# A linear-attention and feed-forward kernel: two cumulative sums a unit instead of three, decays computed two units ahead, and a new order of casts in the ramp

## The chip, the cores and the metric

The kernel runs on one core of a Trainium2 chip. The metric is the device time of one execution in microseconds (us), as the median of several executions. A profile is one execution seen by the hardware profiler. Its engines are PE (TensorE, matrix products), DVE (VectorE), ACT (ScalarE), POOL (GpSimd) and SP, whose queue issues the DMA transfers. Each engine works through its own queue in order. PEld is PE's loading of weights, and the *granted clock* is the share of full speed that PE was granted in the record. In the kernels the results of PE land in tiles of PSUM, and the other tiles lie in SBUF; an *eviction* is an instruction that copies a tile from PSUM to SBUF.

## The reference, cut to what matters

A recurrent attention with a decay per channel is followed by a feed-forward layer with a tanh-gelu. There are 4 batches, 8 heads, 768 steps and a head width of 48.

```python
for t in range(S):                               # r, k, v, w: [4, 8, 768, 48]
    cur = einsum('bhd,bhe->bhde', u[None] * kt, vt)
    y[:, :, t] = einsum('bhd,bhde->bhe', rt, state + cur)
    state = wt[:, :, :, None] * state + einsum('bhd,bhe->bhde', kt, vt)
x = y.transpose(0, 2, 1, 3).reshape(3072, 384)
return gelu_tanh(x @ w_in) @ w_out               # w_in 384 x 2048, w_out 2048 x 384
```

## The kernel before

The work is cut into 12 *units*. A unit is 256 steps of one batch, and two neighbouring steps share a partition. A unit's attention turns the logarithms of the decays into cumulative sums (a matrix product with a triangular matrix), and these into factors by Exp. It multiplies k and r by the factors, transposes both on PE, and forms masked scores, outputs and a new state. Its feed-forward part is an *up-projection* (`mm1`: eight groups of six 256-column matmuls, each group followed by a gelu) and a *down-projection* (`mm2`: two halves of sixteen 384-column matmuls). The attention of unit q+1 is a Python generator whose steps (`next(att)`) are placed between the matmuls of unit q. The preparation of a unit's factors and of its scaled k and r (`kk`, `rq`) is placed at the end of a pass of the loop. POOL prepares `rk` (the product of k, r and u), `vb` (v in bf16), `vsc` (`vb` scaled) and `am` (a block mask scaled by the unit's decay). How many units ahead of its use a preparation is made I call its *lead*; it is one here.

```python
def a1(q):                                # cumulative sums: three for the two steps of a partition
    x, y, z = (ps_a.tile([P, 512], FP, tag="a", name=f"cum{q}_{i}") for i in range(3))
    for dst, s0, s1 in ((x, strict, strict), (y, incl, strict), (z, incl, incl)):
        PE.matmul(dst[:, 0:HD], s0, lw[:, 0, :, 0:D], start=True, stop=False)
        PE.matmul(dst[:, 0:HD], s1, lw[:, 1, :, 0:D], start=False, stop=True)
    ...
def exps(q): ...                          # four Exps of 384 columns, one small one for al
def prep(q):
    DVE.tensor_tensor(out=kk[:, :, :, 0:D], in0=tdh(kt), in1=dec(e1), op=AL.mult)   # 768 columns
    DVE.tensor_tensor(out=rq[:, :, :, 0:D], in0=tdh(rt), in1=dec(fq), op=AL.mult)   # 768 columns
    POOL.tensor_copy(out=vb, in_=tdh(vt))
    POOL.tensor_tensor(out=rk, ...k, r...); POOL.tensor_tensor(out=rk, ...rk, u_bc...)
    for c2 in range(2):
        POOL.tensor_tensor(out=am[:, c2], in0=blk..., in1=al..., op=AL.mult)
def prep_b(q):                            # dg: DVE reduces rk; vsc: POOL multiplies vb by dg
    ...
def a2(q, which):                         # eight PE transposes, then one DVE copy PSUM -> SBUF (TT)
    ...
# ---- ramp (cut): casts of w_in between the steps of attention(0); a1/exps/prep of unit 1 after them
for q in range(NU):
    if q + 3 < NU: load(q + 3, "k"), ...  # loads are issued at the start of the pass
    att = attention(q + 1) ...
    table("gelu")
    if ramp:                              # q < 2: all up-projections first
        for i in range(8): mm1(q, i)
        if q == 0:
            for i in range(8):            # the eight casts of w_out, in one go, over three engines
                cast_w_out(i, DVE if i in (0, 3, 6) else (ACT if i in (1, 4, 7) else POOL))
    for i in range(8):
        if not ramp: mm1(q, i)
        if i >= 2: mm2(q, 0, (2 * i - 4, 2 * i - 3))
        if i in (1, 3, 4, 5, 6, 7): next(att, None)
        if i == 6 and 0 < q and q + 2 < NU: a1(q + 2)
    table("exp")
    ...
    exps(q + 2); ln(q + 3)
    mm2(q, 0, range(12, 16)); ...; store(q, 0)
    prep(q + 2); prep_b(q + 2)            # for the transposes of the next pass
    mm2(q, 1, range(8)); ...; mm2(q, 1, range(8, 16)); store(q, 1)
```

## Time and profile before

The time before is 236.3 us (median of 3 runs, 235.0 to 237.8). The table lists when each unit starts, read from PE's timeline at its first up-projection matmul.

| unit | 1 | 2 | 3 | 4 | 5 | 6 | 7 | 8 | 9 | 10 | 11 | 12 | end |
|---|---|---|---|---|---|---|---|---|---|---|---|---|---|
| start, us | 24.8 | 53.7 | 74.0 | 91.3 | 107.9 | 124.5 | 141.0 | 157.6 | 173.8 | 190.1 | 206.3 | 220.6 | 235.9 |

I call units 1 to 3 the ramp. From unit 4 to unit 9 a unit takes 16.2 to 16.6 us. The page of the kernel before has each engine's busy time and share. It then gives the share of each of 40 equal slices in tenths, and PE's granted clock in tenths:

```profile
span 235.9 us, 5759 instructions
PE 203.4 (86%) x2448; PEld 143.0 (61%) x2448; DVE 131.3 (56%) x211; ACT 134.0 (57%) x223; POOL 104.5 (44%) x87
...
PE   0456787598895999999999999999999999999992
PEclk9999996779997999999999999999999999999998
```

PE is full from the fourteenth slice on; before it, its clock dips twice. The view by stages confirms this. Its columns are the stretch, its length, the busy us and instructions of PE, PEld, DVE, ACT and POOL, then PE's granted clock, and last what the DMA engines did. The two lines are the first unit and the six units from the fourth:

```profile
24.80:53.70 28.90, 21.52 (x209) 13.47 (x207) 19.91 (x21) 16.41 (x27) 18.37 (x14) 0.82 0.80 212
91.30:190.10 98.80, 95.41 (x1235) 68.55 (x1233) 58.94 (x93) 63.12 (x111) 49.31 (x36) 1.00 0.52 117
```

In these six units PE is busy 95.4 of 98.8 us and DVE 58.9 us, which is 9.8 us a unit. The timeline around the start of the seventh unit shows the order on DVE and POOL. Its columns are start, length, engine and line, operation, and the idle time before it with what ended that:

```profile
140.26 0.96 DVE L202 TENSOR_TENSOR kk_126<-k_1635,e_2184 128x768 bf16<-128x768 f32 x1 [0.61 <-ACT e_2184 L184]
...
141.14 0.95 DVE L203 TENSOR_TENSOR rq_128<-r_1637,fq_2183 128x768 bf16<-128x768 f32 x1
141.15 2.42 POOL L215 TENSOR_TENSOR am_2216<-blk,al_2185 128x384 f32<-128x384 bf16 x2 [8.26 <-ACT al_2185 L187]
...
143.34 0.68 DVE L238 COPY TT_1_2278<-T_1_2269 128x1024 bf16<-128x1024 bf16 x1
...
143.75 0.81 PE L345 MATMUL h_2_2291<-xT_2203,w_in_sb 128*128 128x256 bf16 x6 [0.36 <-ACT g_2252 L347]
```

DVE multiplies k and r in 0.95 us each, at once. POOL's two `am` multiplies begin with the second of them and take 2.42 us. In the first unit, where DVE does not multiply two SBUF tiles beside it, each of the pair takes 0.82 us, 1.61 together. The eviction `TT_1` starts 0.4 us after its transposes, behind one copy. PE waits 0.36 us, for a gelu.

### The profile page before, as it was taken

What the parts mean: (1) busy time and instruction counts of PE and PEld (TensorE: products, weight loads), DVE (VectorE), ACT (ScalarE), POOL (GpSimd) and SP (SyncE); (2) the same over time, 40 slices, a digit from 0 to 9 for tenths busy, and PEclk for the clock granted to TensorE, in tenths of its full rate; (3) what the DMA queues carried; (4) which work ended last, traced back from release to release, by engine and by line L of the source; (5) the groups of instructions that cost most, each with busy time, mean ns of one, the idle gap of its engine ahead of it and who ended that gap; (6) DMA issues with size and microseconds to landing.
All of it is one profiled execution on the core that took longest, in us unless ns stands there. A gap on an engine that the chain in (4) does not pass through costs nothing.

```text
span 235.9 us, 5759 instructions
## 1 busy us (share of the span) xinstructions
PE 203.4 (86%) x2448; PEld 143.0 (61%) x2448; DVE 131.3 (56%) x211; ACT 134.0 (57%) x223; POOL 104.5 (44%) x87
## 2 busy tenths in 40 slices
PE   0456787598895999999999999999999999999992
PEld 0334564357564767667767667676777677677761
DVE  7684686561636538547547747656285376374200
ACT  3433780566255449459368377395494684765670
POOL 3473792639008504806708509329158076060000
PEclk9999996779997999999999999999999999999998
DMA  7999999713902911942923914915719120020202
GB/s 173 307 396 297 331 320 255 160 33 72 231 15 54 246 25 36 206 98 53 232 56 75 257 24 111 210 33 124 182 35 212 24 62 10 13 56 0 68 1 67
DMA packets 56969, 30.45 MB, mean 129 GB/s; under 512 B 50928, under 2 KB 56176, under 8 KB 56944
## 3 DMA queue, kind: packets, MB, share of 16 engines
q1 hardware_dynamic: 56944, 30.09, 52.1%
q8 instruction: 19, 0.31, 0.6%
q14 instruction: 6, 0.05, 0.1%
HBM read 25.36 MB, written 4.72 MB: 127 GB/s over the span
## 4 chain that ended last, share of the span: by engine, by line
PE 54%; ACT 19%; DVE 11%; issue 9%; POOL 3%; DMA 2%; DVEq 0%; ACTq 0%; POOLq 0%
ACT L156 5%; DVE w_out_sb L86 2%; DMA w_89<-in_w_dram 2%; PE o_0_532 L354 1%; DVE rq_127 L203 1%; ACT logw_124 L162 1%; PE o_0_3678 L354 1%; PE o_0_3457 L354 1%; PE o_0_3175 L354 1%; PE o_1_3740 L354 1%; PE o_1_3632 L354 1%; PE o_1_3389 L354 1%; POOL rk_418 L210 1%; POOL rk_418 L212 1%; ACT logw_122 L162 1%
## 5 line engine op out<-in xcount | busy, mean ns | idle before, releaser
L345 PEld LDWEIGHTS <-w_in_sb 128*128 128x128 bf16 x576 | 54.0, 99 | 21.1 <-issue 9.9
L156 ACT ACT_TABLE_LOAD x13 | 16.7, 1283 | 0.9 <-PEq L487 0.7
L158 ACT ACT_TABLE_LOAD x12 | 15.4, 1283 | 0.2
L171 PEld LDWEIGHTS <-strict 128*128 128x128 bf16 x24 | 2.5, 104 | 9.9 <-issue 9.5
L215 POOL TENSOR_TENSOR am_997<-blk,al_975 128x384 f32<-128x384 bf16 x2 | 2.4, 1230 | 12.5 <-ACT al_975 L187 12.5
L215 POOL TENSOR_TENSOR am_1304<-blk,al_1273 128x384 f32<-128x384 bf16 x2 | 2.4, 1229 | 11.5 <-ACT al_1273 L187 11.5
L215 POOL TENSOR_TENSOR am_1608<-blk,al_1577 128x384 f32<-128x384 bf16 x2 | 2.4, 1230 | 8.3 <-ACT al_1577 L187 8.3
L215 POOL TENSOR_TENSOR am_1912<-blk,al_1881 128x384 f32<-128x384 bf16 x2 | 2.4, 1230 | 8.3 <-ACT al_1881 L187 8.3
L215 POOL TENSOR_TENSOR am_2216<-blk,al_2185 128x384 f32<-128x384 bf16 x2 | 2.4, 1230 | 8.3 <-ACT al_2185 L187 8.3
L215 POOL TENSOR_TENSOR am_2520<-blk,al_2489 128x384 f32<-128x384 bf16 x2 | 2.4, 1228 | 8.3 <-ACT al_2489 L187 8.3
L215 POOL TENSOR_TENSOR am_2811<-blk,al_2780 128x384 f32<-128x384 bf16 x2 | 2.4, 1228 | 7.9 <-ACT al_2780 L187 7.9
L215 POOL TENSOR_TENSOR am_3100<-blk,al_3069 128x384 f32<-128x384 bf16 x2 | 2.4, 1228 | 7.9 <-ACT al_3069 L187 7.9
L215 POOL TENSOR_TENSOR am_3382<-blk,al_3352 128x384 f32<-128x384 bf16 x2 | 2.4, 1228 | 7.9 <-ACT al_3352 L187 7.9
L354 PE MATMUL o_0_532<-w_out_sb,g_437 128*128 128x384 bf16 x16 | 5.5, 469 | 0.2 <-ACT w_out_sb L84 0.2
L236 PEld LDWEIGHTS <-rq_127 128*128 128x128 bf16 x48 | 3.4, 104 | 3.3 <-DVE rq_127 L203 3.2
L354 PEld LDWEIGHTS <-g_437 128*128 128x128 bf16 x32 | 3.3, 117 | 3.2 <-issue 2.5
L170 PE MATMUL cum_0_201<-logw_122,strict 128*128 128x384 bf16 x1 | 0.5, 479 | 5.4 <-ACT logw_122 L162 5.4
L362 DVE COPY ob_3736<-o_0_3678 128x384 f32<-128x384 f32 x1 | 0.6, 558 | 7.7 <-PE o_0_3678 L354 7.7
L215 POOL TENSOR_TENSOR am_699<-blk,al_677 128x384 f32<-128x384 bf16 x2 | 2.3, 1187 | 4.3 <-ACT al_677 L187 4.3
L354 PEld LDWEIGHTS <-g_3653 128*128 128x128 bf16 x32 | 3.0, 98 | 1.7 <-ACT g_3653 L347 0.4
L238 DVE COPY TT_1_818<-T_1_809 128x1024 bf16<-128x1024 bf16 x1 | 0.7, 692 | 6.0 <-PE T_1_809 L236 6.0
L354 PE MATMUL o_0_3678<-w_out_sb,g_3653 128*128 128x384 bf16 x16 | 3.8, 327 | 0.0
(942 smaller groups left out, 694.2 us busy)
## 6 DMA issues: line engine op xcount, KB each, us to landing
wi_155<-in_moe_w_in_dram SPq DMA_DIRECT2D x1, 512.0 KB, 5.0
wi_157<-in_moe_w_in_dram SPq DMA_DIRECT2D x1, 512.0 KB, 6.0
wi_159<-in_moe_w_in_dram SPq DMA_DIRECT2D x1, 512.0 KB, 6.7
wi_161<-in_moe_w_in_dram SPq DMA_DIRECT2D x1, 512.0 KB, 7.5
wi_163<-in_moe_w_in_dram SPq DMA_DIRECT2D x1, 512.0 KB, 8.7
wi_165<-in_moe_w_in_dram SPq DMA_DIRECT2D x1, 512.0 KB, 9.6
w_89<-in_w_dram SPq DMA_DIRECT2D x1, 384.0 KB, 3.7
k_91<-in_k_dram SPq DMA_DIRECT2D x1, 384.0 KB, 4.7
```

The lines of the kernel that those rows point to most:

```text
L86: eng.tensor_copy(out=out, in_=in_)
L156: ACT.preload_act_table_set(EXP_SET)
L158: ACT.preload_act_table(AF.Gelu_apprx_tanh)
L162: ACT.activation(out=lw[:, :, :, 0:D].rearrange("p t h d -> p h t d"), in_=ld.pop(("w", q)).rearrange("p h (t d) -> p h t d", t=2), func=A ...
L171: PE.matmul(dst[:, 0:HD], s1, lw[:, 1, :, 0:D], start=False, stop=True)
L203: DVE.tensor_tensor(out=rq[:, :, :, 0:D], in0=tdh(rt), in1=dec(fq), op=AL.mult)
L210: POOL.tensor_tensor(out=rk, in0=kt.rearrange("p h (t d) -> p h t d", t=2), in1=rt.rearrange("p h (t d) -> p h t d", t=2), op=AL.mult)
L212: POOL.tensor_tensor(out=rk, in0=rk, in1=u_bc[:, :, None, :].broadcast_to([P, H, 2, D]), op=AL.mult)
L215: POOL.tensor_tensor(out=am[:, c2], in0=blk.rearrange("p g j d -> p g (j d)"), in1=al[:, :, c2][:, :, None].broadcast_to([P, G, 2 * D]), o ...
L236: PE.transpose(ps[:, g, :, t2, :], src[:, t2, ds(2 * g, 2), :], ident)
L345: PE.matmul(h[:, f, :], w_in_sb[:, cb, ts(ft, P)], xT[:, cb, :], start=(f + cb == 0), stop=(cb == NCB - 1), skip_group_check=True)
L354: PE.matmul(st["o", q, c2], g[:, ft, ts(c2, P)], w_out_sb[:, ft, :], start=(ft == 0), stop=(ft == NFT - 1))
```

## The change

The intent is less work a unit and a smoother ramp. The factor between the two steps of a partition is multiplied into k and r directly (`kw`, `rw`), so two cumulative sums and two Exps of 384 columns suffice. Each of the two 768-column multiplies becomes two of 384, and two more make `kw` and `rw`. Decays and preparation run two units ahead, not one. The transposes come right after the first up-projection group. The casts of `w_out` are strung out between PE's work in the first unit, and loads of k, r and v are issued after a unit's stores. The diff, cut to its core:

```diff
-        x, y, z = (ps_a.tile(...) for i in range(3))
-        for dst, s0, s1 in ((x, strict, strict), (y, incl, strict), (z, incl, incl)):
+        x, z = ((pool or ps_a).tile(...) for i in range(2))
+        for dst, tri in ((x, strict), (z, incl)):
...
+    def prep_w(q):
+        DVE.tensor_tensor(out=kw, in0=kt[:, :, 0:D], in1=wt[:, :, D:2 * D], op=AL.mult)
+        DVE.tensor_tensor(out=rw, in0=rt[:, :, D:2 * D], in1=wt[:, :, 0:D], op=AL.mult)
+    def prep_a(q):                       # POOL: rk, rk, and v's cast (on ACT for the first unit)
...
     def prep(q):
-        DVE.tensor_tensor(out=kk[:, :, :, 0:D], in0=tdh(kt), in1=dec(e1), op=AL.mult)
-        DVE.tensor_tensor(out=rq[:, :, :, 0:D], in0=tdh(rt), in1=dec(fq), op=AL.mult)
+        for dst, t2, x, dec in ((kk, 0, kw, e1), (kk, 1, kt[:, :, D:2 * D], e1),
+                                (rq, 0, rt[:, :, 0:D], fq), (rq, 1, rw, fq)):
+            DVE.tensor_tensor(out=dst[:, :, t2, :, 0:D], in0=gjd(x), in1=dec..., op=AL.mult)
...
+    for q in range(3):                   # the ramp: six up-projection groups, transposes, two more
+        ...
+        table("exp")
+        if q == 0: wo(0)                 # wo(i) casts a part of w_out, on ACT and DVE in turn
+        mm2(q, 0, (0, 1))
+        next(att)
+        if q == 0: wo(1)
+        mm2(q, 0, (2, 3))
+        next(att)
+        if q == 0: prep_b(1); wo(2); wo(3)
+        mm2(q, 0, range(4, 8))
+        ...                              # and so on to wo(7)
+    for q in range(3, NU):
+        att = attention(q + 1) if q + 1 < NU else iter(())
+        table("gelu")
+        n = q + 3
+        for i in range(8):
+            mm1(q, i)
+            if i >= 4: mm2(q, 0, (2 * i - 8, 2 * i - 7))
+            if i in (0, 1, 2, 4, 5, 6, 7): next(att, None)
+            if q == 3 and i == 0: prep_a(5)
+            if q == 3 and i == 3: prep_w(5); prep(5); prep_b(5)
+            if n < NU:
+                if i == (4 if q == 3 else 0): prep_a(n)
+                if i == 5: prep_w(n)
+                if i == 6: a1(n); prep_b(n)
+        table("exp")
+        if n < NU: exps(n)
+        ...
+        store(q, 0)
+        if n < NU: prep(n)
+        mm2(q, 1, range(16))
+        store(q, 1)
+        krv(q + 4)                       # loads of k, r, v, behind the stores
```

In code `q` and `n` count from 0, in the text units count from 1.

## The prediction

> **What bounds it now.** Two regimes. (1) From the fourth unit on, TensorE: the timeline shows first up-projection matmuls at 124.5, 141.0 and 157.6 us, a period of 16.56 us, and the table of windows has PE busy 15.8 of 16.5 us. I sum about 15.9 us of issue in one unit: 5.2 up-projection, 5.2 down-projection, 0.9 transposes of k and r, 1.65 cumulative sums, the rest attention. Sixteen down-projection matmuls of 384 columns take 2.60 us, 163 ns each; the Trainium skill ("TensorE: Matmul & The Clock Gate", Back-to-back issue gap) gives N/2.4+2.5 = 162.5 ns, so PE runs warm and tight. Remaining gaps in the timeline: about 0.5 us where the third up-projection waits for the first gelu behind exp, ln and a table load, and 0.31 us where a cumulative sum waits for ScalarE to free a PSUM buffer. (2) The first 91 us (first up-projection at 24.8 us, fourth unit at 91.3) are a dependency chain across all engines: only three units in 66.5 us.
>
> **What changes, costed.** Steady unit: two cumulative sums instead of three remove two 384-column matmuls (0.32 us PE); the Exps fall from four to two (2 x 0.38 us ScalarE), so ScalarE reaches the first gelu before PE needs it and the 0.5 us gap goes. But the transposes now stand between the first and second up-projection, so the score matmuls wait for VectorE's two 0.68 us evictions: I estimate a new 0.5 us gap. The PSUM wait stays. VectorE gains about 1 us a unit, off the path. Period about 15.95 us: -0.55 us for six units.
>
> Decays two units ahead move one unit's sums and exps from the late stage into the ramp: the last two overlapped units run at about 14.6 us.
>
> Ramp: all weight casts of w_in come after the first attention; w_out casts follow the gelus and the exp table load, then alternate with the mask multiplies on VectorE, and PE's in-order queue waits for each. In the first unit v's cast on ScalarE holds up the first exps until v lands (9.0 us). I add up: first gelu about 28.4 us (27.6 before), second unit starts near 58.5 us (53.7), third 75.7 (74.0), fourth 93 (91.3). VectorE multiplies of two SBUF inputs block behind GpSimd (the skill, "SBUF — State Buffer", Summary: rules for kernel authors): one took 2.56 instead of 0.95 us at 26.35 us. The extra multiplies enlarge this in the ramp.
>
> **Sum.** 93 + 6 x 15.95 + 2 x 14.6 + 15.1 = 233 us of span, 233.5 us of time, 1.2% faster. Range 229.5 to 238.5. Chances: faster by over 2% 0.25, within 2% 0.67, slower 0.08.
>
> **What would show each step.** PE's timeline: period 15.8 to 16.1 us; no wait for gelu before the third up-projection, but a wait of score matmuls on VectorE's eviction; second cumulative sum waiting on ScalarE's xs. Fourth unit starts at 91 to 95 us; second unit later than before. Windows: VectorE busy about 11 us per unit, ScalarE about 0.8 us less.
>
> **What would make it wrong.** The ramp: it is a long chain; if VectorE and GpSimd collide less or casts arrive earlier, the fourth unit could start at 88 us and the result pass -2%. If loads of k, r, v, now issued after the stores, land too late, steady units gain nothing.

## The result, and the profile after

The changed kernel takes 261.1 us (median of 4 fast runs, 260.1 to 262.4), the kernel before 236.1 us (235.0 to 237.8) in the same rounds. The ratio is 1.1055, with a 95% interval from 1.097 to 1.114: 10.6% slower. A ratio here is always the mean time of one kernel's runs over that of the other's of the same rounds, so it is not quite the ratio of the medians.

```profile
span 258.4 us, 5726 instructions
PE 202.6 (78%) x2424; PEld 143.5 (56%) x2424; DVE 173.8 (67%) x261; ACT 126.5 (49%) x201; POOL 101.7 (39%) x84
...
PE   1264684547999989939899597798896996999993
PEclk9999996555999999977999999799999999999998
```

The totals of PE, ACT and POOL fell a little; that of DVE rose by 42.5 us with only 50 more instructions. The starts of the units tell where the span went:

| unit | 1 | 2 | 3 | 4 | 5 | 6 | 7 | 8 | 9 | 10 | 11 | 12 | end |
|---|---|---|---|---|---|---|---|---|---|---|---|---|---|
| start, us | 28.0 | 66.7 | 83.4 | 100.2 | 123.0 | 139.4 | 157.8 | 177.6 | 194.7 | 212.4 | 228.6 | 243.2 | 258.4 |
| its unit takes | 38.7 | 16.7 | 16.8 | 22.8 | 16.4 | 18.4 | 19.8 | 17.1 | 17.7 | 16.2 | 14.6 | 15.2 | |
| longer than before | 9.8 | -3.6 | -0.5 | 6.2 | -0.2 | 1.9 | 3.2 | 0.9 | 1.4 | 0.0 | 0.3 | -0.1 | |

The last row and the 3.2 us of the later first start add up to the 22.5 us. There are four places.

**The first unit (+9.8 us).** The view by stages for the first unit, the fourth, and the fifth to ninth:

```profile
28.00:66.70 38.70, 25.70 (x215) 15.62 (x215) 15.82 (x24) 16.44 (x26) 10.54 (x9) 0.69 0.65 177
...
100.20:123.00 22.80, 17.94 (x207) 12.51 (x206) 22.12 (x27) 10.54 (x17) 17.69 (x13) 0.85 0.37 83
123.00:212.40 89.40, 77.17 (x1017) 56.85 (x1015) 73.51 (x97) 48.27 (x79) 42.16 (x30) 0.98 0.47 106
```

In the first unit no engine but PE is busy for half the time, and PE's clock averages 0.69. PE's timeline has the waits in it:

```profile
40.56 0.48 PE L376 MATMUL o_0_526<-w_out_sb,g_437 128*128 128x384 bf16 x2 [2.84 <-ACT w_out_sb L84]
...
43.24 0.80 PE L376 MATMUL o_0_526<-w_out_sb,g_437 128*128 128x384 bf16 x2 [1.84 <-DVE w_out_sb L86]
...
47.32 0.80 PE L376 MATMUL o_0_526<-w_out_sb,g_437 128*128 128x384 bf16 x2 [1.95 <-DVE w_out_sb L86]
...
53.81 0.80 PE L376 MATMUL o_0_526<-w_out_sb,g_437 128*128 128x384 bf16 x2 [2.91 <-DVE w_out_sb L86]
```

The first down-projection waits for a cast again and again. A cast stands in DVE's queue behind mask multiplies that need PE's score matmuls, and those stand in PE's queue behind the down-projection that needs the cast before. The two engines take turns. The two 384-column matmuls at 43.24 end 0.80 us after the first began, against 0.48 us at 40.56: the clock has fallen. PE is busy 4.2 us longer than in the kernel before (25.70 for 21.52) and idle 5.6 us longer; `e6` below shows what the slower matmuls have to do with it.

**The fourth unit (+6.2 us).** Its pass holds two preparations: the sixth unit's, and that of the seventh. DVE is busy 22.1 of its 22.8 us. In DVE's timeline six multiplies of the sixth unit stand in front of the state update of the fifth:

```profile
106.81 1.17 DVE L188 TENSOR_TENSOR rw_1471<-r_1061,w_766 128x384 f32<-128x384 f32 x1
107.90 1.18 DVE L236 TENSOR_TENSOR kk_127<-kw_1470,e_1309 128x384 bf16<-128x384 f32 x1
...
112.48 1.57 DVE L327 TENSOR_TENSOR S_0_1552<-tmp_0_1553,am_1332 128x384 bf16<-128x384 f32 x1
```

PE waits for that `S_0_1552` for 4.6 us, up to 114.10. Four of the six multiplies take 1.16 to 1.18 us, where 0.55 us is what they take undisturbed.

**The fifth to ninth unit (+7.2 us).** DVE is busy 73.5 us in these five units, 14.7 us a unit against 9.8 before. A look at 152 us shows what the added time is:

```profile
152.42 2.01 POOL L197 TENSOR_TENSOR rk_2030<-rk_2030,u_bc 128x768 f32<-128x768 f32 x1
154.37 1.15 POOL L86 CAST vb_2029<-v_1993 128x768 bf16<-128x768 f32 x1
...
152.68 2.16 DVE L187 TENSOR_TENSOR kw_2191<-k_1989,w_1690 128x384 f32<-128x384 f32 x1
154.76 1.17 DVE L188 TENSOR_TENSOR rw_2192<-r_1991,w_1690 128x384 f32<-128x384 f32 x1
```

The same `kw` multiply takes 0.55 us in the units where POOL is idle beside it (`kw_740`, at 67.4 us). Here it ends 0.41 us after POOL's multiply ended, and `rw` 0.41 us after POOL's cast ended. POOL's cast takes 1.15 us against 0.82 us elsewhere in the same trace. The two queues block each other in turn: in these lines each multiply pays for one GpSimd instruction. This is the rule of the Trainium skill, "SBUF — State Buffer", Summary: rules for kernel authors: when VectorE "has two SBUF inputs while the GpSimd op reads SBUF, the second one to issue **fully blocks** until the first finishes". The trace agrees. Note that it shows the block as a long instruction, 2.16 for 0.55 us, not as a wait.

What PE sees of it comes at the start of the next unit, 157.8 us:

```profile
157.65 1.22 DVE L236 TENSOR_TENSOR kk_127<-kw_2191,e_2249 128x384 bf16<-128x384 f32 x1
...
158.41 2.24 POOL L241 TENSOR_TENSOR am_2271<-blk,al_2250 128x384 f32<-128x384 bf16 x2
...
158.79 1.18 DVE L236 TENSOR_TENSOR kk_127<-k_1989,e_2249 128x384 bf16<-128x384 f32 x1
...
159.89 1.18 DVE L236 TENSOR_TENSOR rq_128<-r_1991,fq_2248 128x384 bf16<-128x384 f32 x1
...
161.00 0.55 DVE L236 TENSOR_TENSOR rq_128<-rw_2192,fq_2248 128x384 bf16<-128x384 f32 x1
...
162.53 0.68 DVE L254 COPY TT_1_2323<-T_1_2324 128x1024 bf16<-128x1024 bf16 x1
...
163.26 0.24 PE L271 MATMUL mt_0_0_2347<-TT_1_2323,TT_0_2312 48*64 48x128 bf16 x2 [3.10 <-DVE TT_1_2323 L254]
```

Four multiplies for a unit that needs them a whole pass later stand in DVE's queue ahead of two evictions that PE needs at once. The transposes of `TT_1` were done at 159.5 us. The eviction came 3.0 us later, before it took 0.4.

There is a feedback as well. Loads are now issued behind the stores, and the stores wait for DVE's copies. The list of waits has POOL idle for 8.0 to 8.8 us in five units until r lands, for instance (columns: who waited for what, us in total, times, longest):

```profile
POOL rk_2335 L195 <- DMA r_2296<-in_r_dram: 8.1, 1, 8.1
```

So POOL's `rk` comes late, just where DVE updates the state and multiplies `kw` and `rw`.

**The start (+3.2 us).** The start of the first up-projection moves from 24.8 to 28.0 us. v's cast for the first unit is now on ACT ahead of the first Exp and waits until v has landed at 9.0 us; the first Exp starts at 9.7 us, before at 6.9. In the same stretch several multiplies of DVE are long. The first Exp and two of these multiplies, from the timelines of ACT and DVE:

```profile
9.72 0.47 ACT L218 ACTIVATE e_231<-cum_1_212 128x384 bf16<-128x384 f32 x1
...
11.18 2.16 DVE L236 TENSOR_TENSOR rq_128<-r_93,fq_230 128x384 bf16<-128x384 f32 x1
...
25.33 2.12 DVE L327 TENSOR_TENSOR S_1_394<-tmp_1_395,am_244 128x384 bf16<-128x384 f32 x1
```

Which of the two costs the 3.2 us is settled by `e3` below.

### The profile page after: what moved, and what is told of

Same layout as the page of the kernel before. It is cut to its first block, busy times and chain, and to the rows that moved or that the text cites. A ratio compares the mean times of both kernels' runs of the same rounds, so it can differ in the third digit from the quotient of the medians.

```text
span 258.4 us, 5726 instructions
## 1 busy us (share of the span) xinstructions
PE 202.6 (78%) x2424; PEld 143.5 (56%) x2424; DVE 173.8 (67%) x261; ACT 126.5 (49%) x201; POOL 101.7 (39%) x84
## 4 chain that ended last, share of the span: by engine, by line
DVE 28%; PE 20%; DMA 6%; issue 4%; POOL 2%; SPq 1%; ACT 0%; DVEq 0%; POOLq 0%; ACTq 0%
DVE kk_127 L236 3%; DVE rq_129 L236 2%; DVE rq_128 L236 2%; DMA r_2601<-in_r_dram 2%; DVE kk_126 L236 2%; DMA w_1995<-in_w_dram 2%; DMA w_1690<-in_w_dram 2%; DVE kk_125 L236 2%; PE o_1_3754 L376 1%; PE o_0_3708 L376 1%; PE o_0_3529 L376 1%; PE o_0_3286 L376 1%; PE o_1_3646 L376 1%; PE o_1_3403 L376 1%; DVE kw_3078 L187 1%
## 5 line engine op out<-in xcount | busy, mean ns | idle before, releaser
L367 PEld LDWEIGHTS <-w_in_sb 128*128 128x128 bf16 x576 | 54.9, 101 | 15.2 <-DVE w_in_sb L86 2.0
L157 ACT ACT_TABLE_LOAD x13 | 16.7, 1283 | 0.9 <-PEq L589 0.7
L159 ACT ACT_TABLE_LOAD x12 | 15.4, 1283 | 0.2
L376 PE MATMUL o_0_526<-w_out_sb,g_437 128*128 128x384 bf16 x16 | 6.0, 486 | 10.9 <-DVE w_out_sb L86 6.7
L376 PEld LDWEIGHTS <-g_437 128*128 128x128 bf16 x32 | 3.5, 119 | 14.6 <-issue 13.9
L207 POOL TENSOR_TENSOR vsc_575<-vb_424,dg_574 128x768 bf16<-128x768 bf16 x1 | 1.7, 1663 | 16.3 <-DVE dg_574 L206 16.3
L384 DVE COPY ob_3750<-o_0_3708 128x384 f32<-128x384 f32 x1 | 0.6, 557 | 7.7 <-PE o_0_3708 L376 7.7
L384 DVE COPY ob_716<-o_1_720 128x384 f32<-128x384 f32 x1 | 0.6, 558 | 7.5 <-PE o_1_720 L376 7.5
L195 POOL TENSOR_TENSOR rk_2640<-k_2599,r_2601 128x768 f32<-128x768 f32 x1 | 2.1, 2119 | 8.8 <-DMA r_2601<-in_r_dram 8.8
L207 POOL TENSOR_TENSOR vsc_1336<-vb_1323,dg_1335 128x768 bf16<-128x768 bf16 x1 | 1.5, 1482 | 9.3 <-DVE dg_1335 L206 9.3
L195 POOL TENSOR_TENSOR rk_1725<-k_1684,r_1686 128x768 f32<-128x768 f32 x1 | 1.8, 1810 | 8.3 <-DMA r_1686<-in_r_dram 8.3
L195 POOL TENSOR_TENSOR rk_2030<-k_1989,r_1991 128x768 f32<-128x768 f32 x1 | 1.9, 1897 | 8.0 <-DMA r_1991<-in_r_dram 8.0
L195 POOL TENSOR_TENSOR rk_2930<-k_2891,r_2893 128x768 f32<-128x768 f32 x1 | 1.8, 1827 | 8.1 <-DMA r_2893<-in_r_dram 8.1
L195 POOL TENSOR_TENSOR rk_2335<-k_2294,r_2296 128x768 f32<-128x768 f32 x1 | 1.8, 1813 | 8.1 <-DMA r_2296<-in_r_dram 8.1
L207 POOL TENSOR_TENSOR vsc_757<-vb_744,dg_756 128x768 bf16<-128x768 bf16 x1 | 1.5, 1482 | 8.8 <-PE h_5_810 L367 8.8
L253 PEld LDWEIGHTS <-kk_125 128*128 128x128 bf16 x32 | 2.4, 107 | 4.3 <-DVE kk_125 L236 4.3
L376 PEld LDWEIGHTS <-g_1368 128*128 128x128 bf16 x32 | 3.5, 111 | 2.0 <-issue 0.7
L241 POOL TENSOR_TENSOR am_753<-blk,al_691 128x384 f32<-128x384 bf16 x2 | 1.6, 828 | 7.5 <-ACT al_691 L220 7.5
L253 PEld LDWEIGHTS <-rq_128 128*128 128x128 bf16 x48 | 3.2, 104 | 2.4 <-DVE rq_128 L236 2.4
L376 PE MATMUL o_0_1493<-w_out_sb,g_1368 128*128 128x384 bf16 x16 | 4.5, 405 | 0.0
```

Source lines behind the costliest of these rows:

```text
L157: ACT.preload_act_table_set(EXP_SET)
L159: ACT.preload_act_table(AF.Gelu_apprx_tanh)
L195: POOL.tensor_tensor(out=rk, in0=kt.rearrange("p h (t d) -> p h t d", t=2), in1=rt.rearrange("p h (t d) -> p h t d", t=2), op=AL.mult)
L207: POOL.tensor_tensor(out=vsc, in0=vb, in1=dg.rearrange("p h t -> p t h")[:, :, :, None].broadcast_to([P, 2, H, D]), op=AL.mult)
L241: POOL.tensor_tensor(out=am[:, c2], in0=blk.rearrange("p g j d -> p g (j d)"), in1=al[:, :, c2][:, :, None].broadcast_to([P, G, 2 * D]), o ...
L253: PE.transpose(ps[:, :, g, t2, :], src[:, g, t2, :, :], ident)
```

## The experiments

The theory: the arithmetic is cheaper for PE and ACT, but DVE's multiplies meet POOL's reads, take two to four times as long, and stand in DVE's queue ahead of what PE needs. In the first unit the interleaved casts do the same to PE. The rivals: the arithmetic itself costs the time; the late loads cost it; or the second preparation in the fourth unit and its place do. Runs called one look are one execution and so of unknown state; they are read here by unit durations, and single totals are compared only with large differences. The kernel before, run beside them on the same chip, took 237.2 us (235.6 to 238.1, 7 runs) for `e1`, `e3`, `e4` and `e7`; 237.6 us (236.1 to 238.7, 7 runs) for `e5`, `e6`, `e9` and `e10`; and 236.3 us (one run) for `e8` and `e11`.

### e1_prep5_later: the extra preparation of the fourth pass two groups later

```diff
-            if q == 3 and i == 3:
+            if q == 3 and i == 5:
                 prep_w(5); prep(5); prep_b(5)
```

> One line moves: the preparation of unit 5 in the loop's first pass is issued two steps later, behind the state update instead of ahead of it on VectorE. If the 4.56 us wait of TensorE for the state tile S_0_1552 is a matter of queue order, the first pass of the loop (22.8 us from 100.2 to 123.0) falls to 17 to 18.5 us and the time to 255 to 257 us (from 261). If instead it is the late loads or a slow VectorE in general that hold that pass, it stays above 21 us and the time above 259 us.

Measured, one look: 263.8 us, no gain. The 4.6 us wait for the state is gone, but the next up-projection now waits 3.77 us for `xT`, and the fourth and fifth unit take 19.3 and 23.6 us (22.8 and 16.4 in the changed kernel). The expected fall did not come: moving the double preparation moves the wait, so its place alone is not the cause. Whether its amount is, this run can't say; `e3` can.

### e3_pool_writes_only: GpSimd no longer reads SBUF beside DVE

This kernel is wrong (relative error 46,696): POOL's multiplies and casts are replaced by a one-column instruction and memsets of the full tile.

```diff
-        POOL.tensor_tensor(out=rk, in0=kt..., in1=rt..., op=AL.mult)
-        POOL.tensor_tensor(out=rk, in0=rk, in1=u_bc..., op=AL.mult)
+        POOL.tensor_tensor(out=rk[:, 0:1, 0, 0:1], in0=kt[:, 0:1, 0:1], in1=rt[:, 0:1, 0:1], ...)
+        for _ in range(2):
+            POOL.memset(rk, 0.01)
     ...                                  # the same for vb (from the second unit on), vsc and am
```

> Wrong results on purpose: GpSimd's multiplies and cast become memsets of the same tiles (two per multiply), with a one-column multiply kept so that the same loads and tiles are waited for. GpSimd then writes SBUF and hardly reads it. If VectorE's long multiplies are blocked by GpSimd's reads, all of its 384-column multiplies fall to 0.55 us (from 1.2 to 2.2 us), VectorE's busy time falls from 174 to about 145 us, units five to nine fall from 16.4 to 19.8 us to about 16 us each, and the whole to 244 to 250 us. If the order of the queues alone makes the waits, the multiplies shorten little and the time stays above 257 us.

Measured, one look: 236.2 us, about as long as the kernel before and less than the 244 to 250 us expected. Every one of DVE's 384-column multiplies takes 0.55 us, DVE's total falls from 173.8 to 138.9 us, the fourth unit takes 16.6 us and the steady ones 15.4. The order of DVE's queue is as in the changed kernel and loads still come late (POOL waits 39.6 us for r in 7 waits), and neither does harm. So the steady loss and the fourth unit's need the collisions: with the same two preparations and nothing blocked, the fourth unit is 1.2 us longer than a steady one. A limit of this run: memsets are also shorter than what they replace, and POOL's total falls from 101.7 to 82.9 us. The first unit still takes 38.2 us, so it has another cause.

The run also settles the start:

```profile
9.71 0.47 ACT L222 ACTIVATE e<-cum 128x384 bf16<-128x384 f32 x1
...
11.16 0.55 DVE L240 TENSOR_TENSOR rq<-r,fq 128x384 bf16<-128x384 f32 x1
...
24.72 0.37 PE L372 MATMUL h<-xT,w_in_sb 128*128 128x256 bf16 x1 [0.65 <-DVE xT L358]
```

v's cast is still on ACT and the first Exp as late as in the changed kernel, but the multiplies are short, and the first up-projection starts at 24.7 us as in the kernel before. So the 3.2 us come from the blocked multiplies, not from the cast.

### e4_loads_first: loads at the start of a pass

```diff
         n = q + 3
+        krv(q + 4)
+        if q + 5 < NU:
+            load(q + 5, "w")
         for i in range(8):
     ...
         store(q, 1)
-        krv(q + 4)
-        if q + 5 < NU:
-            load(q + 5, "w")
```

> The loads of k, r, v and w for a later unit are issued at the start of a unit, ahead of the stores, from the fourth unit on. If late loads (GpSimd waits 8 to 8.8 us for r in six units) are what stretches units six to nine, these fall from 17 to 20 us to about 16.2 us and the time to about 252 us. If the loads only shift GpSimd's work and the collisions with VectorE remain, it stays within 4 us of 261, with the multiplies still at 1.2 us or more.

Measured, one look: 250.1 us. Units six to nine take 15.8 us; the fourth still 22.8 and the fifth 19.5. With r there in time, POOL's `rk` runs early in the pass and no longer meets the state update and the `kw` multiplies (median 0.55 us); the `rq` multiplies still meet `am` (median 1.18 us). The late loads are thus one way in which steady collisions arise, a feedback that the change built in, and not the whole cause.

### e11_evictions_first: the multiplies behind the next pass's evictions

```diff
                 next(att, None)
+            if i == 0 and q > 3 and q + 2 < NU:
+                prep(q + 2)              # behind the transposes and evictions of unit q+1
     ...
         store(q, 0)
-        if n < NU:
-            prep(n)
         mm2(q, 1, range(16))
```

> The changed kernel with the four multiplies and two mask multiplies of a unit two ahead moved from the end of one pass to just behind the two transpose evictions of the next pass; loads, ramp and the fourth unit's double preparation stay. Theory A (the steady units lose time because the blocked multiplies stand ahead of evictions in VectorE's queue): the waits of score matmuls on the second eviction, 2 to 3.3 us in five units, fall under 1 us, units six to nine go from 16.4 to 19.8 us to about 16, total about 252 us, although multiplies of over 1 us remain. Theory B (the late loads cause it, the queue order only shows it): units six to nine stay at 17 to 19 us, another wait takes the place of the evictions, total about 258 us. In both the first unit stays at 38 us and the fourth at 22.8 us.

Measured, one look: 251.0 us, as the first theory said. The loads remain late (POOL waits 38.8 us for r in 6 waits), yet the units from the sixth to the ninth take 16.2 us, and the longest wait of score matmuls on an eviction falls from 3.3 to 0.3 us. The timeline at the start of the seventh unit, to be read against the one at 157.8 us above:

```profile
155.06 1.61 POOL L241 TENSOR_TENSOR am<-blk,al 128x384 f32<-128x384 bf16 x2
...
156.76 1.29 DVE L254 COPY TT<-T 128x1024 bf16<-128x1024 bf16 x2 [0.55 <-PE T L253]
...
157.96 0.55 DVE L236 TENSOR_TENSOR kk<-kw,e 128x384 bf16<-128x384 f32 x1
...
158.10 0.42 PE L271 MATMUL mt<-TT,TT 48*64 48x128 bf16 x16 [0.28 <-DVE TT L254]
```

The evictions come first. Since the multiplies come later, POOL's `am` is also done before they begin, in 1.61 us and not 2.24, and `kk` takes 0.55 us. So this run takes away the order and one collision together. It refutes late loads as the sole cause. `e3` (same order, no collisions, no loss) shows that the order alone costs nothing; whether blocked multiplies would do harm behind the evictions, this run doesn't show, for they are no longer blocked there. The collision of `rk` with state update and `kw` remains here, and these units are 0.8 us longer than the 15.4 us of `e3`.

### e7_arithmetic_only: the new arithmetic in the old schedule

The ramp, the loop and the lead of one unit are those of the kernel before; sums, Exps, multiplies and layouts are the changed ones.

```diff
-            prep(q + 2)                  # the loop of before
-            prep_b(q + 2)
+            prep_w(q + 2)
+            prep(q + 2)                  # four multiplies of 384 columns
+            prep_a(q + 2)
+            prep_b(q + 2)
```

> The kernel before, its ramp, its loop and one unit of lead, with only the arithmetic of the change: two cumulative sums, w folded into half of k and r on VectorE, two exps instead of four. If the schedule is what costs 25 us, this is 233 to 238 us, about the kernel before, with a period of 16.0 to 16.6 us. If the arithmetic itself (six VectorE multiplies with two SBUF inputs for two) is what costs, the period rises above 17.5 us and the time above 245 us.

Measured, three rounds: 246.1 us (245.3 to 247.0, 4 runs), ratio 1.0385 (1.032 to 1.045). The first unit starts at 29.4 us and takes 28.1, so its 38.7 us come from the new ramp order. Steady units take 17.1 us against 16.56: six multiplies, two of them at 1.18 us, now stand between the Exps and the transposes where two stood. The saved matmuls and Exps do not pay for that in the old place. Neither expectation holds as a whole: the time is above 245 us, but the period stays under 17.5 us, and 4.6 us of the loss are the start, where three multiplies take 1.18, 2.16 and 2.16 us. What the new arithmetic needs is another place; `e9` gives it one by computing the Exps a unit earlier.

### e6_wo_casts_first: all casts of w_out in one go

```diff
+        if q == 0:
+            for i in range(8):
+                wo(i)
         table("exp")
-        if q == 0:
-            wo(0)
         mm2(q, 0, (0, 1))
         next(att)
-        if q == 0:
-            wo(1)
     ...                                  # and the others likewise
```

> Only the eight w_out casts of the first unit move: they are issued together after the gelus, ahead of the exp table load and of the mask multiplies. If the first unit's 38.7 us come from TensorE waiting in turn for casts queued behind attention's work (waits of 2.8, 1.8, 2.0, 2.9 and 1.3 us), it falls to 29 to 33 us and the time to 253 to 256 us. If the loads of w_out are late themselves, the first unit stays above 36 us.

Measured, one look: 252.3 us. The first unit takes 28.9 us, 9.8 us less than in the changed kernel and as long as before. Of the waits for casts one of 1.42 us is left.

```profile
28.15:57.09 28.94, 21.56 (x215) 14.11 (x215) 15.27 (x24) 16.36 (x26) 10.39 (x9) 0.88 0.89 237
```

Against the line of the changed kernel, PE has as many matmul records (215) in 4.1 us less busy time, at a clock of 0.88 instead of 0.69, and 5.6 us less idle time. This shows the interleaving of casts to be the cause of the first unit's loss. Later units keep their losses.

### e5_start: v's cast on POOL, second sums later, two w_in casts earlier

```diff
-        cast(ACT if q == 0 else POOL, vb, tdh(vt))       # behind rk
+        if q < 2: POOL.tensor_copy(out=vb, in_=tdh(vt))  # ahead of rk
     ...
     next(att)
-    a1(1, ps_h, "h")
     next(att)
     next(att)
+    a1(1, ps_h, "h")
     prep_b(0)
+    cast_w_in(0, ACT)
     exps(1)
+    cast_w_in(1, ACT)
     ...                                  # their old places removed
```

> Only the start is changed back in part: v's cast goes to GpSimd and ahead of its multiplies for the first two units (as before), the second unit's cumulative sums come after the score matmuls of the first, and two w_in casts are done on ScalarE before the first attention ends. If the start was lost to v's cast holding up ScalarE and to VectorE blocked behind GpSimd (2.0 and 2.2 us multiplies at 7.8 and 11.2 us), the first up-projection moves from 28.0 to 24.5 to 26 us and everything after by about as much; time 256 to 259 us. If the start is bound by loads or by something else, the first up-projection stays above 27 us.

Measured, one look: 261.0 us. The first up-projection starts at 26.3 us (28.0), but the second unit at 64.8 us (66.7) and the total is the same: `kw` of the second unit now meets POOL and takes 2.16 us (1.18), and later units, slowed by the same collisions, swallow the rest. Start and total both lie outside what was expected. The first Exp starts at 7.0 us, but three multiplies behind it still take 1.18, 2.16 and 2.16 us. By itself the run is inconclusive; with `e3` it says that moving the cast, with the multiplies still blocked, wins back only 1.7 of the 3.2 us.

### e9_prep_one_ahead: sums two ahead, multiplies one ahead

```diff
-            if q == 3 and i == 0: prep_a(5)
-            if q == 3 and i == 3: prep_w(5); prep(5); prep_b(5)
-            if n < NU:
-                if i == (4 if q == 3 else 0): prep_a(n)
-                if i == 5: prep_w(n)
-                if i == 6: a1(n); prep_b(n)
+            if i == 0 and q + 2 < NU: prep_a(q + 2)
+            if i == 5 and q + 2 < NU: prep_w(q + 2); prep(q + 2)
+            if i == 6 and n < NU: a1(n)
+            if i == 6 and q + 2 < NU: prep_b(q + 2)
     ...
-        if n < NU:
-            prep(n)
         mm2(q, 1, range(16))
```

> From the fourth unit on, exps stay two units ahead, but the preparation (w into k and r, the decay multiplies, GpSimd's products) runs for the next but one unit only, in the middle of a unit behind the state update, instead of for the one after it at the unit's end; no pass prepares two units. If collisions of VectorE with GpSimd in front of the transposes' evictions and late loads make the stretched units, all units from the fourth fall to 15.3 to 16 us (22.8 and 16.4 to 19.8 now) and the time to 238 to 243 us, with VectorE's multiplies near 0.55 us. If VectorE is simply too full, the period stays above 16.5 us.

Measured, one look: 238.7 us. The fourth unit and all steady ones take 15.4 us, and no pass holds a second preparation. POOL's and DVE's timelines from the sixth unit:

```profile
134.97 1.62 POOL L241 TENSOR_TENSOR am<-blk,al 128x384 f32<-128x384 bf16 x2
...
140.57 0.55 DVE L187 TENSOR_TENSOR kw<-k,w 128x384 f32<-128x384 f32 x1
141.04 0.55 DVE L188 TENSOR_TENSOR rw<-r,w 128x384 f32<-128x384 f32 x1
141.51 0.55 DVE L236 TENSOR_TENSOR kk<-kw,e 128x384 bf16<-128x384 f32 x1
```

POOL finishes its four reads early in the pass, at 136.6 us, and DVE multiplies from 140.6 us, with POOL idle. The evictions at the start of the pass have nothing in front of them.

### e10_all: e5, e6 and e9 together

The edit is the sum of the three above.

> The start, the w_out casts and the preparation of the three runs before together. If their gains lie in different stretches and add, 224 to 231 us, faster than the kernel before by 2 to 5 per cent; if they are the same time counted twice, 233 us or more.

Measured, three rounds: 226.0 us (225.2 to 229.5, 5 runs, one of them, 229.5, over 1.5% above the fastest); ratio to the kernel before 0.949 (0.943 to 0.956). This beats both kernels, by 5.1% and by some 35 us. The first unit starts at 26.3 us and takes 30.2; then come 16.7 and 16.8, six of 15.4, and 14.5 us. The page, of an execution of 228.5 us:

```profile
span 226.8 us, 5737 instructions
PE 196.0 (86%) x2424; PEld 140.7 (62%) x2424; DVE 145.9 (64%) x260; ACT 126.8 (56%) x201; POOL 94.4 (42%) x85
```

DVE does the same multiplies as in the changed kernel in 145.9 us, 27.9 us less. From the fifth to the ninth unit it is busy 10.8 us a unit. So the change's arithmetic costs DVE about 1 us a unit over the 9.8 us before, as I had counted, and another 3.9 us in the changed kernel was blocking.

### e8_start_casts_loads: the same, but keeping the lead of two units

The edits of `e5`, `e6` and `e4` together.

> The changed kernel with three edits tried before, together: the new start, the w_out casts first, and the loads issued before the stores; the lead of two units stays. If the times of the units add up from the single runs: first up-projection 26.3 us, first unit about 30, second and third 16.7 and 16.8, fourth 22.8, fifth 19.5, then 15.8 to the last two of 14.7; total about 239 us, 12 to 13 us over the version with a lead of one unit (226.0), of which 11 us lie in the fourth and fifth unit. If the lead of two is harmless once the ramp is mended, the fourth and fifth unit fall to 16 us and the total to 229 us or less.

Measured, one look: 242.0 us, near the sum. First unit 29.1 us; fourth and fifth 21.4 and 22.0 us; then 15.8. In the fourth unit PE waits 4.5 us for the state, and in the fifth 4.2 us for an eviction, behind four multiplies of 1.2, 1.2, 1.2 and 2.15 us. Mending ramp and loads does not repair the pass with two preparations; a lead of one unit for the multiplies does.

## Why the prediction was wrong

I predicted 233.5 us; the chip gave 261.1. The error lies in these steps. The predicted span was 233 us, the measured one 258.4 us.

| step of the sum | predicted, us | measured, us | miss, us |
|---|---|---|---|
| start of the fourth unit | 93 | 100.2 | +7.2 |
| six units from the fourth | 6 x 15.95 = 95.7 | 112.2 | +16.5 |
| next two units | 29.2 | 30.8 | +1.6 |
| last unit | 15.1 | 15.2 | +0.1 |

**The main failed step: "VectorE gains about 1 us a unit, off the path."** The work was sized well, as `e10` showed (10.8 against 9.8 us). But I had named the collision only for the ramp ("The extra multiplies enlarge this in the ramp") and costed the steady multiplies undisturbed. In the changed kernel DVE spent 14.7 us a unit. It was not off the path either: I had placed the evictions behind the transposes and estimated "a new 0.5 us gap", without what stands ahead of them in DVE's queue. The waits came where I had put them, but not for my reason: they were 2.0 to 3.3 us in five units and 1.2 in one, and the evictions' own length was not what made them. Without collisions (`e3`) or with the multiplies placed elsewhere (`e9`, `e11`) no such wait of PE was over 0.3 us.

**The fourth unit.** I gave it 15.95 us like the others and so overlooked that a lead grown from one to two must be paid for in one pass, with two preparations. It took 22.8 us, a miss of about 7 of the 16.5 us. `e1` and `e8` show that neither another place nor earlier loads help; `e9` shows that leaving it out does. `e3` shows what of it is work and what is blocking: with both preparations unblocked the unit takes 16.6 us, so most of the 7 us is once more the multiplies' blocked time.

**The ramp.** I wrote that "PE's in-order queue waits for each" cast, and put the second unit at 58.5 us. It came at 66.7 us. The mechanism was right and the term mis-sized, by 8.2 us: PE stood in four waits for casts of 1.8 to 2.9 us and a fifth of 1.3 us, 10.8 us in all, and ran at a clock of 0.69 on average, half-speed in between. `e6` gives 9.8 us of the unit back. For the start I had named v's cast and put the first gelu 0.8 us later. The start came 3.2 us later, and `e3` shows this to be blocked multiplies, which I had named for the ramp ("enlarge this in the ramp") without adding a number for them. The second and third unit took 16.7 and 16.8 us, where I had 17.2 and 17.3.

**Late loads.** These stood among what would make it wrong ("land too late, steady units gain nothing"). They came late, and `e4` and `e11` show how they worked: not by PE waiting for them, but by moving POOL's reads onto DVE's multiplies.

**What held.** The gelu wait at the third up-projection vanished. ScalarE fell by 0.87 us a unit (10.52 to 9.65), for about 0.8 predicted. The unit's PE work is even less than I thought: 15.4 us undisturbed for 15.95. The wait of a cumulative sum on ScalarE, which I said would stay, is absent from PE's list of waits. The Trainium skill, "TensorE: Matmul & The Clock Gate", Back-to-back issue gap, gives N/2.4 + 2.5 ns for warm and N/1.2 for cold matmuls of N columns, as the gap of an isolated matmul, and says that the warm formula is too long for a stream at large N; for six of 256 columns it gives, as an estimate, 0.66 and 1.28 us. The trace agrees with the formula, even in a stream (163 ns each in sixteen of 384 columns): groups in the first unit start 1.28 us apart in the changed kernel (29.78, 31.06, 32.34 us, where the view still gives a clock of 1.00) and 0.66 us in the kernel before (29.74, 30.40 us). My sum held no slow matmuls in the ramp. With the waits for casts removed, `e6` saves 5.6 us of idle time and 4.1 us of PE's busy time, so these waits were paid for twice.

**What stays open.** The order of DVE's queue alone costs nothing (`e3`), but what blocked multiplies would cost behind the evictions can't be said: whichever run moved the multiplies also moved them away from POOL's `am`. `e3` also shortened POOL's own work, and apart from `e7` and `e10` the runs are single. Why the first groups of a unit in the ramp run at half speed at a recorded clock of 1.00 is open.

## What to carry to other kernels

When a change gives VectorE more instructions with two SBUF inputs, don't cost them at their undisturbed time: look up what GpSimd reads at the same moment, and place the two in different parts of the loop. Ask of every in-order queue what the new work stands in front of; work that is needed a pass later must come behind evictions that are needed now. When a lead is lengthened, find the pass that pays for it, and where weights are cast, finish the casts before the first consumer instead of letting two engines take turns.

## What the Trainium skill lacked or had wrong

- "SBUF — State Buffer", Who interferes with whom, states the lock for one pair of instructions. It lacks what two queues of such instructions do to each other: they alternate, and each multiply pays for a whole GpSimd instruction (0.55 us became 1.17 us behind v's cast and 2.16 us behind a 768-column multiply), while GpSimd's pair of `am` multiplies went from 1.61 to 2.24 us.
- The same page has no word on how a block looks in a profile: it is inside the instruction's busy time, not a wait. DVE's busy total rose by 42.5 us, 27.9 us of which went away in `e10` with the same multiplies.
- "ScalarE: Activation LUTs", What ACT_TABLE_LOAD costs, gives 1283 ns for the load and 1380 ns of drain, 2.66 us for every switch. The load is 1283 ns in both traces, but the drain is not to be seen: in the kernel before, the load at 141.81 us starts 0.01 us after the Ln ahead of it ended and is followed by the first gelu at 143.10 us, 1.29 us later.
